# The last unit of a seven-product output matmul: products in banks of their own, the last product by row tile over two banks

## The chip, the cores and the metric

The kernel runs on one core of one Trainium2 chip. The metric is the device time of one execution in microseconds (us), as the median of nine runs; lower is better. One further execution was taken by the hardware profiler, and all durations below come from it. The engines are named as the profile names them: PE (TensorE matmuls), PEld (its weight loads), DVE (VectorE), ACT (ScalarE), POOL (GpSimd) and SP (SyncE, which here only issues DMAs).

## What is computed

```
kv  = einsum('bhsd,bhse->bhde', k, v)            # batch 8, heads 8, seq 576, head_dim 64
o   = einsum('bhsd,bhde->bhse', q, kv)
x   = o / sqrt(mean(o*o) + 1e-6) * g_norm        # -> 4608 tokens x 512
a   = x @ w_a ; b = x @ w_b                      # d_ff 1536
out = (a * b) @ w_out                            # 4608 x 512, float32
```

Only the last line, for the last 512 tokens, concerns the change.

## The kernel before, in words

**Tiling.** The 4608 tokens go in nine blocks of 512. The first block is done with plain matmuls; the eight others use a seven-product scheme (a Winograd form of Strassen's) for both halves of the feed-forward part. `wino_block` makes `a*b` for a block (lines 789 to 897, its matmuls recorded at L839), and `o_block`/`o_unit` (914 to 1109, matmuls at L1008) multiply `a*b` by `w_out`. The output work of block i-1 is mixed with the `a`, `b` work of block i. After the last block only its own output work is left; it is one unit of 512 tokens, which takes the branch `if W:` of `o_unit` (line 1065). That branch is all that the change touches.

**The unit.** Its `a*b` (tile `abt`) is cut in four: the first and second 256 tokens, and the upper and lower half of d_ff. `w_out` (tile `wo`) is cut in four too. DVE makes the sums of blocks at L993 (into `as`, or in place in `abt`); the sums of `w_out` lie in `so`. The seven products p1 to p7 are 256 x 256 outputs, each of two row tiles of 128 tokens ("subs" 0 and 1, written p3[0] and p3[1] below), each row tile six matmuls of 128x256. So a product is 12 matmuls and the unit 84. A product's two row tiles fill the two halves of a PSUM bank (512 fp32 columns). The four quarters of the output are

```
c11 = p1 + p2                    U2 = p1 + p6       U3 = U2 + p7
c22 = U3 + p5      c21 = U3 + p4      c12 = U2 + p5 + p3
```

Operands tell the products apart in the profile: p1, p2 and p5 are `wo,abt`; p4 is `so,abt`; p6 and p7 are `so,as`; p3 is `wo,as`.

**How the sums are made before the change.** Bank X holds p1; ACT copies it out (e1, L1040); p6 is accumulated in the same bank, which makes U2, and ACT copies that out (e2); then p7 is accumulated there too, which makes U3, and ACT copies that out (e3). Bank Z holds p5; ACT copies it to `u` (e5, L1076), then p3 is accumulated on it. DVE adds (function `comb`, all at L1046): c11 from bank Y and e1; c22 from bank X and `u`; c12 from bank Z and e2; c21 from two banks W[0], W[1], one per row tile, and e3. p4 alone is run by row tile. `put` issues the stores: 128 rows by 256 columns (128 KB) each, eight in the unit, on SP's or ACT's queue.

**What sets the order.** Every step is a node with an engine, a planned duration, a priority and dependences. `Plan.order` (lines 104 to 134) works through planned time: each engine takes the node of the smallest priority number among those that are ready within 0.06 us, else the one that is ready first. The result is emitted as one program per engine, and an engine runs its program strictly in that order. In this unit a product's priority is `pr + off*du`, with `off` the first argument of `prod`, and its matmuls are nodes of two (`pieces` is `NJ // 2`, 3 per row tile), so a later product can fill a gap left by an earlier one. Buffers come from rings with a limit: RO is bank 4; RX and RY share banks 0 to 3, two each; RQ and RS share banks 5 to 7, two each. `RU` gives the six `u` buffers. The unit's rings stand in the last call, lines 1153 to 1156.

**Stores.** The stores of the last unit are issued by `store` (L911). Each is one DMA over all 16 DMA engines.

Of the kernel before, what the change touches and what calls it, by code (L numbers as in the profile page):

```python
# [137 lines left out]
def kernel(  # L138
# [11 lines left out]
    nc = tc.nc  # L150
# [31 lines left out]
    NJ = FC // 2  # L182
    OP = 2
    EH = d_model // 2
# [221 lines left out]
    def mm_us(n, cols):  # L406
        return n * (cols / 2400 + 0.0025)

    def act_us(n, bias=False):
        return (0.155 if bias else 0.06) + n / 1200  # L410

    def dve_us(n):
        return (n + 65) / 960
# [7 lines left out]
        ]  # L421

    T0 = 20.0
    B5, B6, CX, CY = 5, 8, 3, 4
    TB, TURN, AHEAD = 5, 3.0, 8.0
    plan = Plan({"PE": 5.7, "DVE": 3.3, "ACT": 2.7, "SP": 5.0, "POOL": 22.5, "V": 0.0})
# [5 lines left out]
    RX, RY, RO = Ring(PB, 2), Ring(PB, 2), Ring(PO)  # L432
    RQ, RS = Ring(PA, 2), Ring(PA, 2)
    RU, RB, RAB = Ring([u_t[:, i] for i in range(6)]), Ring(b_ts), Ring(ab_ts)
# [464 lines left out]
    def store(g0, o_sb, queue=None, es=slice(0, d_model)):  # L899
        queue = queue or nc.sync  # L900
        i = 0
        while i < 128:
            b, j = divmod(g0 + i, S)
            if b < NE:
                c, sp = divmod(j, EP)
                n = min(128 - i, EP - sp)
                r0, st = b * S + EC * sp + c, EC
            else:
                n = min(128 - i, S - j)
                r0, st = b * S + j, 1  # L910
            queue.dma_start(out=out[r0 : r0 + st * (n - 1) + 1 : st, es], in_=o_sb[i : i + n, es])  # L911
            i += n
# [54 lines left out]
    def o_unit(r0, ab, muls, osum, pr, du, chunks, pieces, m, w, first, second, X, Y, Z, ob, s2, s3, s4, W):  # L967
# [3 lines left out]
        def a(lo, cols):  # L971
            return lambda js: ab.tile[:, js.start + (0 if lo else NJ) : js.stop + (0 if lo else NJ), cols]

        def sx(b):
            return lambda js: b.tile[:, js, 0:w]

        a11, a12, a21, a22 = a(1, first), a(0, first), a(1, second), a(0, second)
# [21 lines left out]
        def prod(off, ps, lhs, rhs, start, deps, takes=(), frees=(), need=None, subs=None):  # L999
            last, first = [], (subs or slice(0, m)).start  # L1000
            step = NJ // pieces
            for sub in range(m)[subs or slice(0, m)]:
                for pc in range(pieces):
                    js = range(pc * step, (pc + 1) * step)

                    def mm(sub=sub, js=js):
                        for j in js:
                            nc.tensor.matmul(  # L1008
                                ps.tile[:, sub * EH : (sub + 1) * EH],
                                lhsT=lhs(slice(j, j + 1))[:, 0, sub * 128 : (sub + 1) * 128],  # L1010
                                rhs=rhs[:, j, :],
                                start=start and sub == first and j == 0,
                                stop=j == NJ - 1,
                                skip_group_check=True,
                            )

                    nd = [muls[x] for j in js for x in (j, j + NJ) if x in muls]
                    if need is not None:
                        nd = [done[need, q] for q in range(js[0] // cj, js[-1] // cj + 1)]
                    last = [  # L1020
                        plan.add(
                            "PE", mm_us(len(js), EH), pr + off * du + 0.01 * sub, mm,
                            last + list(deps) + nd, takes if not last else (), list(frees) + [ab],
                        )
                    ]
            return last[0]

        def bank(b, subs):
            n = subs.stop - subs.start
            return b.tile[:, subs.start * EH : subs.stop * EH].rearrange("p (s e) -> p s e", s=n)  # L1030

        every = slice(0, m)

        def o(fi, h, subs=every):
            return ob.tile[:, fi * m + subs.start : fi * m + subs.stop, h * EH : (h + 1) * EH]

        def ev(off, fi, h, dep, takes=(), frees=()):
            return plan.add(
                "ACT", act_us(m * EH), pr + off * du,
                lambda: nc.scalar.copy(o(fi, h), bank(X, every)), [dep], takes, frees,  # L1040
            )

        def comb(off, fi, h, ps, deps, frees=(), subs=every, u=None):
            def add():
                other = u.tile[:, subs] if u else o(fi, h, subs)
                nc.vector.tensor_add(o(fi, h, subs), bank(ps, subs), other)  # L1046

            return plan.add(
                "DVE", dve_us((subs.stop - subs.start) * EH), pr + off * du, add, deps, (), frees
            )  # L1050

        def put(fi, subs, deps, us=0.45, queue="SP", es=slice(0, d_model)):
            q = {"SP": nc.sync, "ACT": nc.scalar}[queue]

            def go():
                for i in range(subs.start, subs.stop):
                    store(r0 + (fi * m + i) * 128, ob.tile[:, fi * m + i], q, es)

            plan.add(queue, us * (subs.stop - subs.start), pr + 7 * du, go, deps, (), [ob])

        b11, t1 = wo_t[:, 0:NJ, 0:EH], wo_t[:, 0:NJ, EH:]
        b21, b22 = wo_t[:, NJ:, 0:EH], wo_t[:, NJ:, EH:]
        t2, t3, t4 = (so_t[:, i] for i in range(3))
        n1, n2, n3, n4 = osum
        if W:
            u5 = Buf(RU)
            p1 = prod(0, X, a11, b11, True, [], [X])
            e1 = ev(0, 0, 0, p1, [ob])
            p2 = prod(1, Y, a12, b21, True, [], [Y])
            c11 = comb(1, 0, 0, Y, [p2, e1], [Y])  # L1070
            p6 = prod(2, X, sx(s2), t2, False, [e1, n2], (), [s2], 2)
            e2 = ev(2, 0, 1, p6)
            p5 = prod(3, Z, a21, t1, True, [n1], [Z], (), 1)
            e5 = plan.add(
                "ACT", act_us(m * EH), pr + 3 * du,
                lambda: nc.scalar.copy(u5.tile[:, every], bank(Z, every)), [p5], [u5],  # L1076
            )
            p7 = prod(4, X, sx(s3), t3, False, [e2, n3], (), [s3], 0)
            e3 = ev(4, 1, 0, p7)
            c22 = comb(4, 1, 1, X, [p7, e5], [X, u5], u=u5)  # L1080
            p3 = prod(5, Z, sx(s4), b22, False, [e5, n4], (), [s4], 3)
            c12 = comb(5, 0, 1, Z, [p3, e2], [Z])
            e1s, e2s = slice(0, EH), slice(EH, d_model)
            put(0, every, [c11], es=e1s)
            put(1, every, [c22], es=e2s)
            for i in range(m):
                put(0, slice(i, i + 1), [c12], queue=("SP", "ACT")[i], es=e2s)
            for i in range(m):
                subs = slice(i, i + 1)
                p4 = prod(6 + 0.1 * i, W[i], a22, t4, True, [n4], [W[i]], subs=subs)  # L1090
                c21 = comb(6 + 0.1 * i, 1, 0, W[i], [p4, e3], [W[i]], subs)
                put(1, subs, [c21], queue=("ACT", "SP")[i], es=e1s)
            return
        p1 = prod(0, X, a11, b11, True, [(wo_n, 10.6)], [X])
        e1 = ev(0, 0, 0, p1, [ob])
# [2 lines left out]
        p6 = prod(2, X, sx(s2), t2, False, [e1, n2], (), [s2], 2)  # L1098
        e2 = ev(2, 0, 1, p6)
        p5 = prod(3, Z, a21, t1, True, [e1, n1], [Z], (), 1)  # L1100
        p7 = prod(4, X, sx(s3), t3, False, [e2, n3], (), [s3], 0)
        e3 = ev(4, 1, 1, p7)
        c22 = comb(4, 1, 1, Z, [p5, e3])
        p4 = prod(5, X, a22, t4, False, [e3, n4])
        c21 = ev(5, 1, 0, p4, (), [X])
        p3 = prod(6, Z, sx(s4), b22, False, [c22], (), [s4], 3)
        c12 = comb(6, 0, 1, Z, [p3, e2], [Z])
# [6 lines left out]
    n_at = [1.2, 1.0, 1.0, 1.0, 1.0, 1.0, 1.0, 1.0, 0.5]  # L1114
    st = [T0]
    for i in range(len(lens)):
# [24 lines left out]
    for bi in range(1, nb + 1):  # L1141
# [10 lines left out]
        ab, muls = wino_block(bi, (st[bi], st[bi + 1]), wsum)  # L1152
    o_block(
        nb, ab, muls, osum, (st[nb + 1], st[nb + 1] + o_us[nb]), NJ // 2,
        (RO, RY, RY, RS, RQ), NJ // 2,
    )
    order, t = plan.order(), 5.7
    for n in order:
# [34 lines left out]
```

## Time and profile before

| what | us |
|---|---|
| median of 9 runs | 296.97 (296.83 to 298.78) |
| the profiled execution, own time | 296.97 |
| its span in the trace | 294.8 |
| last matmul run of the unit ends | 289.85 |
| last store issued | 291.32 |

A profile row reads: start, duration, engine, line of the kernel, operation, output<-inputs, shapes, count and, in brackets, how long the engine had been idle and who released it. Matmuls overlap: a row of several begins at its first and ends with its last, and neighbouring rows overlap by about 0.16 us. SPq and ACTq rows are DMA issues on those queues. `bk` is a PSUM bank, `o_sb` the output tile in SBUF that is stored from. The "chain that ended last" is followed backwards from the program's last instruction.

### The profile page before, as it was taken

Reading aid. Unit: us, or ns where it says so; the run is one execution under the profiler, and the core shown is the slowest. Engines: PE = TensorE matmul, PEld = TensorE weight load, DVE = VectorE, ACT = ScalarE, POOL = GpSimd, SP = SyncE. Lnnn points to the kernel's source line nnn. Section 1 sums busy time; section 2 is a strip of 40 time slices with the busy share of each in tenths; the row PEclk is TensorE's granted clock in tenths of the full one; section 3 lists DMA queues with packets and bytes.
Section 4 is the critical chain, followed back from the end, with each engine's and each line's share of the span. In section 5 each row is a group of like instructions: output and inputs, shape, how many; then the busy total and the mean of one; then the engine's idle time right before and its main releaser. Section 6 shows DMA issues by size and latency. Waiting matters only on the chain.

```text
span 294.8 us, 6759 instructions
## 1 busy us (share of the span) xinstructions
PE 287.4 (97%) x2648; PEld 237.7 (81%) x2648; DVE 240.1 (81%) x441; ACT 191.7 (65%) x395; POOL 77.4 (26%) x96
## 2 busy tenths in 40 slices
PE   7999999999999999999999999999999999999993
PEld 3645558965888888899988999898988888888882
DVE  5454879893987988789979999979989958798852
ACT  3756667776578677877757866786769546665420
POOL 8944830950091470470001910000000000000000
PEclk9999999999999999999999999999999999999999
DMA  8999999799999999699716999330155001200053
GB/s 180 198 199 199 197 158 166 104 168 184 198 120 170 140 174 176 50 142 203 167 30 149 147 165 167 80 145 21 37 88 164 2 0 41 104 2 0 9 172 107
DMA packets 112643, 36.26 MB, mean 123 GB/s; under 512 B 89060, under 2 KB 108516, under 8 KB 112612
## 3 DMA queue, kind: packets, MB, share of 16 engines
q0 software_dynamic: 77552, 18.44, 66.0%
q1 hardware_dynamic: 34448, 16.70, 26.7%
q10 hardware_dynamic: 612, 0.71, 0.8%
q8 instruction: 20, 0.33, 0.4%
q14 instruction: 11, 0.09, 0.1%
HBM read 37.75 MB, written 14.75 MB: 178 GB/s over the span
## 4 chain that ended last, share of the span: by engine, by line
PE 88%; DVE 4%; DMA 3%; POOL 2%; issue 1%; ACT 1%; DVEq 0%; ACTq 0%; POOLq 0%
PE bk L839 47%; PE bk L1008 24%; PE bk L387 7%; PE bk L943 3%; DMA wb_t<-in_moe_w_b_dram 3%; PE bk L624 2%; PE bk L367 1%; PE bk L353 1%; POOL as L242 1%; PE bk L539 1%; DVE c L858 1%; POOL so L242 1%; PE bk L341 1%; DVE so L746 1%; DVE o_sb L1046 1%
## 5 line engine op out<-in xcount | busy, mean ns | idle before, releaser
L858 DVE TENSOR_TENSOR c<-bk,u 128x512 f16<-128x512 f32 x144 | 96.3, 685 | 19.3 <-PE bk L839 11.8
L420 ACT COPY u<-bk 128x512 f32<-128x512 f32 x144 | 81.4, 591 | 36.5 <-PE bk L839 29.9
L839 PE MATMUL bk<-xp,wa_t 128*128 128x256 f16 x288 | 55.0, 273 | 0.1
L839 PE MATMUL bk<-xp,wb_t 128*128 128x256 f16 x288 | 55.0, 273 | 0.0
L839 PEld LDWEIGHTS <-wa_t 128*128 128x128 f16 x384 | 37.1, 98 | 5.7 <-issue 0.3
L1008 PEld LDWEIGHTS <-abt 128*128 128x128 f16 x384 | 37.5, 98 | 4.7 <-issue 0.3
L839 PEld LDWEIGHTS <-wb_t 128*128 128x128 f16 x384 | 37.6, 98 | 4.4
L1008 PE MATMUL bk<-wo_t,abt 128*128 128x256 f16 x288 | 37.2, 273 | 0.1
L839 PE MATMUL bk<-T,sb 128*128 128x256 f16 x192 | 36.7, 273 | 0.0
L839 PE MATMUL bk<-T,sa 128*128 128x256 f16 x192 | 36.6, 273 | 0.0
L420 ACT CAST c<-bk 128x512 f16<-128x512 f32 x48 | 28.0, 587 | 12.1 <-PE bk L839 11.5
L893 DVE TENSOR_TENSOR abt<-c 128x1024 f16<-128x1024 f16 x48 | 32.7, 685 | 0.9
L839 PEld LDWEIGHTS <-sb 128*128 128x128 f16 x288 | 28.2, 98 | 3.3
L839 PEld LDWEIGHTS <-sa 128*128 128x128 f16 x288 | 27.9, 98 | 3.5
L1008 PEld LDWEIGHTS <-as 128*128 128x128 f16 x288 | 28.1, 98 | 3.3
L1040 ACT COPY o_sb<-bk 128x512 f32<-128x512 f32 x31 | 18.2, 586 | 18.5 <-PE bk L1008 18.0
L376 DVE SCALAR_TENSOR_TENSOR xp<-bk,g_col,rs 128x288 f16<-128x288 f32 x40 | 20.3, 513 | 11.1 <-ACT rs L371 11.1
L1008 PE MATMUL bk<-so,as 128*128 128x256 f16 x192 | 25.2, 273 | 0.0
L371 ACT ACTIVATE rs<-bk,eps_t 128x288 f32<-128x288 f32 x40 | 20.0, 506 | 6.5 <-PE bk L367 6.3
L667 POOL DMA_DIRECT2D k_t<-in_k_dram x24 | 21.2, 899 | 0.8 <-issue 0.5
L661 POOL DMA_DIRECT2D scr<-in_q_dram x12 | 19.6, 1638 | 2.7 <-issue 1.5
L1046 DVE TENSOR_TENSOR o_sb<-bk,o_sb 128x512 f32<-128x512 f32 (+1 forms) x25 | 16.4, 664 | 3.0 <-PE bk L1008 2.3
(107 smaller groups left out, 428.2 us busy)
## 6 DMA issues: line engine op xcount, KB each, us to landing
out_dram<-o_sb SPq DMA_DIRECT2D x20, 256.0 KB, 2.7
scr<-in_q_dram POOLq DMA_DIRECT2D x12, 288.0 KB, 7.5
k_t<-in_k_dram POOLq DMA_DIRECT2D x24, 128.0 KB, 7.6
v_t<-in_v_dram POOLq DMA_DIRECT2D x6, 512.0 KB, 10.6
out_dram<-o_sb SPq DMA_DIRECT2D x18, 128.0 KB, 2.4
wa_t<-in_moe_w_a_dram POOLq DMA_DIRECT2D x6, 256.0 KB, 10.8
wb_t<-in_moe_w_b_dram POOLq DMA_DIRECT2D x6, 256.0 KB, 11.0
wo_t<-in_moe_w_out_dram POOLq DMA_DIRECT2D x2, 768.0 KB, 9.3
```

Of the source, the lines that this page charges most:

```text
L371: nc.scalar.activation(rs, self.s_ps[p, h][:, 0:HF], AF.Abs_reciprocal_sqrt, bias=eps_t)
L376: nc.vector.scalar_tensor_tensor(out=xcols(p, self.b * S + h * HF, HF), in0=self.x_ps[p, h][:, 0:HF], scalar=g_col, in1=self.rs[p, h], op0 ...
L387: nc.tensor.matmul(ps[:, 0:n], lhsT=w[:, kc, fc * 128 : (fc + 1) * 128], rhs=xcols(kc, 0, n), start=(kc == 0), stop=(kc == KC - 1),)
L420: ("ACT", act_us(n), lambda: nc.scalar.copy(*args())),
L661: nc.gpsimd.dma_start(out=scr[:, :, hl, :].rearrange("p s d -> s p d"), in_=qv[hl])
L667: nc.gpsimd.dma_start(out=kt[:, c], in_=ks[:, :, c, :])
L839: nc.tensor.matmul(ps.tile[:, i * n : (i + 1) * n], lhsT=lhs(w, sm)[:, kc, :], rhs=rhs()[:, kc, :], start=start and i == 0 and kc == 0, st ...
L858: lambda: nc.vector.tensor_add(cs(fi, h), full(ps), u.tile),
L893: nc.vector.tensor_mul(t, c[:, :, :, 0], c[:, :, :, 1])
L1008: nc.tensor.matmul(ps.tile[:, sub * EH : (sub + 1) * EH], lhsT=lhs(slice(j, j + 1))[:, 0, sub * 128 : (sub + 1) * 128], rhs=rhs[:, j, :], ...
L1040: lambda: nc.scalar.copy(o(fi, h), bank(X, every)), [dep], takes, frees,
L1046: nc.vector.tensor_add(o(fi, h, subs), bank(ps, subs), other)
```

## The change

The rings of the unit become (RO, RY, RS, RY, RS, RQ, RY), so that it has seven banks at hand instead of five.

- p7 no longer accumulates on U2. It starts in a bank V of its own (from RY), with `off` 2.5. ACT's copy e3 is gone; DVE makes U3 as bank V plus e2, into the place in `o_sb` of c21 (new node c2x).
- p5 is run by row tile, into two banks Z[0] and Z[1] (both from RS); ACT copies each half bank, 256 columns, to `u`.
- c22 becomes a DVE sum of two SBUF operands: U3 in `o_sb` and `u`.
- p4 still goes by row tile, into banks from RQ and RY, but with `off` 5 and 5.1 instead of 6 and 6.1. Its sums c21 wait for c22, since they overwrite the U3 that c22 reads.
- p3 goes last (`off` 6 and 6.1) and by row tile, each on its own Z bank; each 256-column piece of c12 is added and stored by itself. Before, c12 was one sum of 512 columns whose two stores followed it.

Matmuls: 84 before and after. Stores: eight before and after.

```
-            p7 = prod(4, X, sx(s3), t3, False, [e2, n3], (), [s3], 0)
-            e3 = ev(4, 1, 0, p7)
-            c22 = comb(4, 1, 1, X, [p7, e5], [X, u5], u=u5)
-            p3 = prod(5, Z, sx(s4), b22, False, [e5, n4], (), [s4], 3)
-            c12 = comb(5, 0, 1, Z, [p3, e2], [Z])
+            u5, V, Z = Buf(RU), W[0], [Z, W[1]]
+            W = W[2:]
...
+            e2 = ev(2, 0, 1, p6, (), [X])
+            p7 = prod(P7_AT, V, sx(s3), t3, True, [n3], [V], [s3], 0)
+            c2x = plan.add(
+                "DVE", dve_us(m * EH), pr + 4 * du,
+                lambda: nc.vector.tensor_add(o(1, 0), bank(V, every), o(0, 1)), [p7, e2], (), [V],
+            )
+            e5 = []
+            for i in range(m):
+                p5 = prod(3 + 0.1 * i, Z[i], a21, t1, True, [n1], [Z[i]], (), 1, subs=rows[i])
+                e5.append(
+                    plan.add(
+                        "ACT", act_us(EH), pr + 3 * du,
+                        lambda i=i: nc.scalar.copy(u5.tile[:, rows[i]], bank(Z[i], rows[i])),
+                        [p5], [] if i else [u5],
+                    )
+                )
+            c22 = plan.add(
+                "DVE", dve_us(m * EH), pr + 4.2 * du,
+                lambda: nc.vector.tensor_add(o(1, 1), o(1, 0), u5.tile[:, every]), [c2x] + e5, (), [u5],
+            )
...
             for i in range(m):
-                put(0, slice(i, i + 1), [c12], queue=("SP", "ACT")[i], es=e2s)
+                p4 = prod(5 + 0.1 * i, W[i], a22, t4, True, [n4], [W[i]], subs=rows[i])
+                c21 = comb(5 + 0.1 * i, 1, 0, W[i], [p4, c22], [W[i]], rows[i])
+                put(1, rows[i], [c21], queue=("ACT", "SP")[i], es=e1s)
             for i in range(m):
-                subs = slice(i, i + 1)
-                p4 = prod(6 + 0.1 * i, W[i], a22, t4, True, [n4], [W[i]], subs=subs)
-                c21 = comb(6 + 0.1 * i, 1, 0, W[i], [p4, e3], [W[i]], subs)
-                put(1, subs, [c21], queue=("ACT", "SP")[i], es=e1s)
+                p3 = prod(6 + 0.1 * i, Z[i], sx(s4), b22, False, [e5[i], n4], (), [s4], 3, subs=rows[i])
+                c12 = comb(6 + 0.1 * i, 0, 1, Z[i], [p3, e2], [Z[i]], rows[i])
+                put(0, rows[i], [c12], queue=("ACT", "SP")[i], es=e2s)
...
-        (RO, RY, RY, RS, RQ), NJ // 2,
+        (RO, RY, RS, RY, RS, RQ, RY), NJ // 2,
```

The change's name also says that q is turned in one piece. No line of the diff touches that: q of each later batch is already turned by one transposing DMA before the change (line 682).

More of the change, by code (lines that the diff above doesn't have):

```diff
@@ L423 @@
     T0 = 20.0
+    P7_AT = 2.5
     B5, B6, CX, CY = 5, 8, 3, 4
@@ L1065, in o_unit @@
         if W:
-            u5 = Buf(RU)
+            u5, V, Z = Buf(RU), W[0], [Z, W[1]]
+            W = W[2:]
+            rows = [slice(i, i + 1) for i in range(m)]
             p1 = prod(0, X, a11, b11, True, [], [X])
@@ L1071, in o_unit @@
             p6 = prod(2, X, sx(s2), t2, False, [e1, n2], (), [s2], 2)
[L1072 to L1076, printed above, removed]
-            )
-            p7 = prod(4, X, sx(s3), t3, False, [e2, n3], (), [s3], 0)
-            e3 = ev(4, 1, 0, p7)
-            c22 = comb(4, 1, 1, X, [p7, e5], [X, u5], u=u5)
-            p3 = prod(5, Z, sx(s4), b22, False, [e5, n4], (), [s4], 3)
-            c12 = comb(5, 0, 1, Z, [p3, e2], [Z])
+            e2 = ev(2, 0, 1, p6, (), [X])
[3 more added lines that the diff above has]
+                lambda: nc.vector.tensor_add(o(1, 0), bank(V, every), o(0, 1)), [p7, e2], (), [V],
+            )
+            e5 = []
[12 more added lines that the diff above has]
+            )
             e1s, e2s = slice(0, EH), slice(EH, d_model)
```

## The prediction, made before the result was known

> **What bounds the kernel now.** I read the page first, for the bound of the whole; then the chain of waits from 255 us on, for what sets the end; then the timeline of the last 14 us, for the order of products; then the stores one by one and the DMA rates of the last 5 us.
>
> ```profile
> PE 287.4 (97%) x2648; PEld 237.7 (81%) x2648; DVE 240.1 (81%) x441; ACT 191.7 (65%) x395; POOL 77.4 (26%) x96
> ```
>
> PE is busy for 97% of the span, so the body is PE's. The unit touched here comes after the body: it can give back only what lies behind the last matmul, or lose by stalling PE. The end of the chain:
>
> ```profile
> 280.46 8.09 PE bk L1008 x74
> ...
> 288.58 0.59 ACT o_sb L1040
> ...
> 289.20 1.02 DVE o_sb L1046 x2
> 290.22 0.33 DVEq L1188
> 290.55 0.60 DVE o_sb L1046
> ```
>
> The chain leaves PE at 288.56, not at PE's end. It goes over ACT's copy e3 and then a queue of four DVE sums (c22, c21[0], c21[1], c12) to 291.15. The timeline of the same stretch shows which products stand there:
>
> ```profile
> 287.07 1.47 PE L1008 MATMUL bk<-so,as 128*128 128x256 f16 x12
> 288.38 1.47 PE L1008 MATMUL bk<-wo_t,as 128*128 128x256 f16 x12
> 288.58 0.59 ACT L1040 COPY o_sb<-bk 128x512 f32<-128x512 f32 x1 [1.16 <-PE bk L1008]
> 289.20 0.69 DVE L1046 TENSOR_TENSOR o_sb<-bk,u 128x512 f32<-128x512 f32 x1 [3.80 <-ACT o_sb L1040]
> ```
>
> p7 (`so,as`) ends at 287.07 + 1.47 = 288.54, e3 starts 0.04 later, c22 0.03 after e3. p3 (`wo,as`) ends at 289.85, but its sum c12 queues behind the three others. DVE was idle for 3.8 us before c22: all four sums pile up behind e3.
>
> The stores pile up too. The first of the last six is issued at 289.91 (behind c22), the last at 291.32. The DMA rates of 289.5 to 294.3 in 40 slices of 0.12 us, then the stores issued about 291.2 to 291.3, then the lone one at 285.4:
>
> ```profile
> GB/s 0 0 0 0 0 0 0 0 0 0 137 350 316 239 290 350 358 324 359 316 316 350 358 324 342 358 333 325 350 333 128 0 0 0 0 0 0 0 0 0
> ```
> ```profile
> DMA to landing us min/median/max: 2.1/2.2/2.3
> ```
> ```profile
> L911 SPq DMA_DIRECT2D out_dram<-o_sb x1: 332/332/332, 285.4 to 285.4; - x1
> ...
> DMA to landing us min/median/max: 1.7/1.7/1.7
> ```
>
> Bytes run without a gap from 290.7 to 293.2, at about 335 GB/s. So the last store lands 2.3 us after its issue, at 293.6, against 1.7 for one with the queue to itself: the tail is a full DMA queue, and its start at c22 matters as much as the last issue. After the landing come about 1.2 us of closing instructions to 294.8, and 2.17 us outside the span make 296.97. Neither is touched.
>
> **The order after the change.** Priorities are in planned time, so I followed the planner's rule by hand. Which gaps a later product fills can be read before the change:
>
> ```profile
> 280.95 0.60 PE L1008 MATMUL bk<-so,abt 128*128 128x256 f16 x4
> 281.39 0.60 PE L1008 MATMUL bk<-wo_t,abt 128*128 128x256 f16 x4
> 281.83 0.38 PE L1008 MATMUL bk<-so,abt 128*128 128x256 f16 x2
> 282.05 0.60 PE L1008 MATMUL bk<-wo_t,abt 128*128 128x256 f16 x4
> ```
>
> These are p4, p2, p4, p5: the last mul of `a*b` (L893) ends only at 282.45, and PE fills up with what needs it not. In the new order p5 has the smaller priority number and its RS banks are free, so it takes p4's slots; p7[0] takes p5's slot at 282.05, when RY has its second bank. Then p1 (8 matmuls), p2 (8), p7[0] (2), p6 (12, from 284.67 as now), p7[1] (6), p5[0] and p5[1] (2 each, to 287.07), p4[0], p4[1], p3[0], p3[1] (6 each). That is 84 matmuls in the same 84 slots of 0.109 us, the last run again ending at 289.85, if PE waits nowhere. The waits that are new on PE, with those who would queue behind them (all the unit's later matmuls, as PE runs in order): p5's first pieces need DVE sums in `abt` that ended by 275.3; p7[0] needs its RY bank, which the former unit's c12 left at 281.85 (margin 0.20, and p5 stood in that slot with the same need); p7's last pieces need the L993 sum that ended at 282.91 (margin 1.5); p3[0] needs e5[0] (below, margin 1.0). I cost them at nothing; each us of stall would cost one.
>
> **Costs part by part**, from these rows:
>
> ```profile
> L640 ACT CAST kvd<-bk 64x256 bf16<-64x256 f32 x6 | 2.2, 368 | 0.1
> ...
> L1046 DVE TENSOR_TENSOR o_sb<-bk,o_sb 128x256 f32<-128x256 f32 x2 | 0.7, 414 | 0.0
> L1046 DVE TENSOR_TENSOR o_sb<-bk,u 128x512 f32<-128x512 f32 x1 | 0.7, 691 | 3.8 <-ACT o_sb L1040 3.8
> ```
>
> Removed: e3, 0.59 us of ACT, all of it in the chain. Added: c2x, a DVE sum of a bank and SBUF, 0.69; one more 256-column piece on each of ACT and DVE.
>
> - c2x: p7[1] ends at 286.80, e2 at 286.77 (as now), so it runs from 286.84 to 287.53, in DVE's 3.8 us of idleness.
> - e5: a 256-column copy on ACT has no row of its own shape. It lies between half of the 512-column copy, 0.29, and the whole, 0.59. I take the 0.37 of the 64x256 cast, the row of the same width. p5[0] ends at 287.01: e5[0] 287.05 to 287.42, e5[1] to 287.79 (to 288.23 at 0.59 each, still inside the slack found below).
> - c22 from two SBUF operands in fp32 is not in the trace. The nearest row has 512 columns with one bank operand, 0.69; the 256-column row (0.414) bounds it from below. I take 0.69: 287.82 to 288.51.
> - c21[0], c21[1]: p4[1] ends at 288.54. Before, two such pieces started 0.33 apart, so c21[0] runs 288.54 to 288.96, c21[1] 288.87 to 289.29. This wait of c21 for c22 is new; behind it on DVE stand c21 and c12 alone.
> - c12[0]: p3[0] ends at 289.20, so 289.24 to 289.65. c12[1]: 289.89 to 290.30.
>
> So the last sum ends at 290.30 instead of 291.15, 0.41 + 0.04 behind the last matmul. c22 has slack: four more sums behind it need 3 x 0.33 + 0.41, so it could end 0.4 later before c12[1] moved.
>
> [...] two halves cost 2 x 0.33 of DVE against 0.61 from c22's start to the next, 0.05 more in throughput. [...] By the rows the piece behind the last matmul is 0.41, and DVE has room for the 0.05. I follow the rows: the split is worth 0.27, not a loss.
>
> **The stores.** Issues, each just behind its sum (SP's second 0.38 behind its first): c22 on SP 288.54 and 288.92, c21[0] on ACT 288.99, c21[1] on SP 289.32, c12[0] on ACT 289.68, c12[1] on SP 290.33. ACT has no copy left to delay. Data began 0.79 after the first issue before (289.91 to 290.70), and 131 KB at 335 GB/s takes 0.39. One behind another: 289.33 to 289.72, then 290.11, 290.50, 290.89, 291.28, 291.67. The queue now drains as fast as it fills, and the last landing is 0.4 behind the last byte (293.61 against 293.2 before), at about 292.1.
>
> Sum: 293.6 - 292.1 = 1.5 us. The profiled execution's own time is 296.97, equal to the median: 296.97 - 1.5 = **295.5**.
>
> [...]
>
> **The rivals.**
> 1. *Only the issue moves.* The last store still takes 2.3: 296.97 - 0.99 = 296.0. For it: the stores at 290.3 took 2.0 to 2.2 with only one or two ahead. Against: 1.7 on an empty queue.
> 2. *PE pays it back.* One of the new waits on PE (V's bank, with 0.2 us of margin, is the tightest) stalls everything by about 1.3 us, or c22 comes late by that and 0.4 more: 296.8, no change. Against: p5 passed in the same slot with no gap, and the e5 margin is 1.0. That the order doesn't come out as I derived it belongs here; p3 and p4 swapped would leave the tail the same.
> 3. *Slower: the sums wait for stores in flight.* c21 and c12 write `o_sb` while c22's stores read it. If writes to one tile waited for its stores, c21[1] would wait for the landing of c22's second store (288.92 + 1.8 = 290.7), end at 291.15, its store land at 293.0, and c12 follow that: its second piece ends at 293.8, its store lands at 295.6, 2.0 later than now: 299.0. It decides when c21[1] starts after 290.2. Against: now c12 starts at 290.47 with three stores from this tile in flight, so regions are told apart.
>
> **How the numbers follow.** 0.2% (0.6 us) is about what a measurement of this kernel can tell from no change. Main case 0.64 (295.2 to 295.75); rival 1 0.20 (295.75 to 296.3); rival 2 0.09; rival 3 0.07. Faster 0.84, within 0.2% 0.09, slower 0.07. The range 295.2 to 296.3 takes in the first two; the low end has the last landing at 1.5 behind its issue, less than any store took.
>
> **What would show it.** Right: no ACT copy behind p7; DVE sums spread from 286.8 to 290.3, the last a 128x256 starting 0.04 behind PE; PE still ending 84 slots after 280.5, with no gap; the last store issued at 290.3 and landing at 292.1. Wrong: a gap in PE's row of the unit, c21[1] after 290.2, a landing 2.3 behind the last issue, or an earlier stage that moved though the diff leaves it alone.

## The result and the profile after

The changed kernel takes 295.77 us as the median of nine runs, against 297.0 for the kernel before on the same chips: ratio 0.9956, 95% interval 0.9946 to 0.9966, so 0.44% faster. In two later sets it took 295.48 and 295.60 beside 297.02 and 297.01. The forecast was 295.5 with a range of 295.2 to 296.3. The profiled execution of the changed kernel took 295.24, with a span of 293.1.

The page's first rows, as before the change: PE is as busy as it was, and DVE has the two instructions more that were counted.

```profile
PE 287.8 (98%) x2648; PEld 237.8 (81%) x2648; DVE 241.1 (82%) x443; ACT 191.1 (65%) x395; POOL 77.3 (26%) x96
```

The chain that ended last now stays on PE until its last matmul and ends with one short sum; line numbers have moved by one, so L1009 is the former L1008.

```profile
280.14 9.40 PE bk L1009 x86
289.54 0.02 issue
289.56 0.42 DVE o_sb L1047
```

The timeline of the unit gives the order of the products (columns: start, duration, engine, line, operation, output<-inputs, shapes, count, idle before; rows that don't bear on the order are left out):

```profile
280.63 1.25 PE L1009 MATMUL bk<-wo_t,abt 128*128 128x256 f16 x10
281.72 0.60 PE L1009 MATMUL bk<-so,as 128*128 128x256 f16 x4
282.16 2.13 PE L1009 MATMUL bk<-wo_t,abt 128*128 128x256 f16 x18
283.45 0.59 ACT L1041 COPY o_sb<-bk 128x512 f32<-128x512 f32 x1 [4.65 <-PE bk L1009]
284.12 2.35 PE L1009 MATMUL bk<-so,as 128*128 128x256 f16 x20
284.38 0.69 DVE L1047 TENSOR_TENSOR o_sb<-bk,o_sb 128x512 f32<-128x512 f32 x1 [0.42 <-PE bk L1009]
285.85 0.59 ACT L1041 COPY o_sb<-bk 128x512 f32<-128x512 f32 x1 [1.81 <-PE bk L1009]
286.31 0.60 PE L1009 MATMUL bk<-wo_t,abt 128*128 128x256 f16 x4
286.56 0.69 DVE L1079 TENSOR_TENSOR o_sb<-bk,o_sb 128x512 f32<-128x512 f32 x1 [1.49 <-PE bk L1009]
286.72 0.65 ACT L1087 COPY u<-bk 128x256 f32<-128x256 f32 x2 [0.29 <-PE bk L1009]
286.74 1.47 PE L1009 MATMUL bk<-so,abt 128*128 128x256 f16 x12
287.40 0.69 DVE L1093 TENSOR_TENSOR o_sb<-o_sb,u 128x512 f32<-128x512 f32 x1
288.05 1.47 PE L1009 MATMUL bk<-wo_t,as 128*128 128x256 f16 x12
288.20 1.13 DVE L1047 TENSOR_TENSOR o_sb<-bk,o_sb 128x256 f32<-128x256 f32 x3
289.56 0.42 DVE L1047 TENSOR_TENSOR o_sb<-bk,o_sb 128x256 f32<-128x256 f32 x1 [0.23 <-PE bk L1009]
```

These are 80 of the unit's 84 matmuls; its first four stand at 279.10. By the kinds of operands the order is the one that was worked out, in slots with no gap: p5[0], p2 and p5[1] (10), p7[0] (4), p5[1], p1 and p2 (18), p7[0], p6 and p7[1] (20), the rests of p5 (4), then p4 and p3. How a row divides among products of the same kind is not in the row itself, but what follows each product starts where this division has it end: e1 behind p1 (283.45), c11 behind p2 (284.38), e2 behind p6 (285.85). c2x (L1079) and c22 (L1093) now run beside p4's matmuls. Three sums are done before the last matmul, and DVE waits 0.23 for the last one.

The DMA rates of 287.5 to 292.3 in slices of 0.12 us, and the store issued last, at 290.05:

```profile
GB/s 0 0 0 0 0 0 0 0 0 0 0 0 222 350 341 171 196 358 324 359 324 358 324 359 324 359 299 367 341 359 324 350 137 9 0 0 0 0 0 0
```
```profile
DMA to landing us min/median/max: 1.8/1.8/1.8
```

The bytes begin at 288.9, 0.6 ahead of the last matmul's end; before, they began 0.9 behind it. They take about as long as before (2.6 against 2.5) and end at 291.5. The last store lands at 291.86.

I measure the end by three distances from the end of the last matmul run: the last issue, the last landing (the *tail*), and the *closing* from there to the end of the span.

| profiled execution | last matmul ends | last issue | tail | closing |
|---|---|---|---|---|
| before | 289.85 | 1.47 | 3.76 | 1.22 |
| after | 289.52 | 0.53 | 2.34 | 1.23 |

So 1.42 of the 1.73 us between these two profiled executions is the tail. The other 0.33 arises before the code that was changed. In both kernels PE waits for the first half of w_b at 16 us, and that load came at different times (PE and its weight load, before and then after):

```profile
16.39 0.11 PEld L387 LDWEIGHTS <-wb_t 128*128 128x128 f16 x2 [0.77 <-DMA wb_t<-in_moe_w_b_dram]
16.39 0.60 PE L387 MATMUL bk<-xp,wb_t 128*128 128x512 f16 x2 [0.28 <-DMA wb_t<-in_moe_w_b_dram]
```
```profile
16.07 0.11 PEld L387 LDWEIGHTS <-wb_t 128*128 128x128 f16 x2 [0.47 <-DMA wb_t<-in_moe_w_b_dram]
16.07 0.61 PE L387 MATMUL bk<-xp,wb_t 128*128 128x512 f16 x2
```

Matmul by matmul, the two executions differ by 0.33 from here on, up to the end.

### The profile page after: what moved, and what is told of

Same layout as the page of the kernel before. It is cut to its first block, busy times and chain, and to the rows that moved or that the text cites. A ratio compares the mean times of both kernels' runs of the same rounds, so it can differ in the third digit from the quotient of the medians.

```text
span 293.1 us, 6763 instructions
## 1 busy us (share of the span) xinstructions
PE 287.8 (98%) x2648; PEld 237.8 (81%) x2648; DVE 241.1 (82%) x443; ACT 191.1 (65%) x395; POOL 77.3 (26%) x96
## 4 chain that ended last, share of the span: by engine, by line
PE 92%; DVE 3%; DMA 1%; issue 1%; ACTq 0%; ACT 0%
PE bk L840 48%; PE bk L1009 25%; PE bk L387 7%; PE bk L944 3%; PE bk L625 2%; PE bk L353 2%; PE bk L367 2%; DMA g_row<-in_g_norm_dram 1%; PE bk L310 1%; PE bk L341 1%; PE bk L540 1%; PE bk L325 1%; DVE c L859 1%; DVE so L747 1%; DVE T L807 1%
## 5 line engine op out<-in xcount | busy, mean ns | idle before, releaser
L1009 PEld LDWEIGHTS <-abt 128*128 128x128 f16 x384 | 37.5, 98 | 4.6 <-issue 0.3
L1009 PE MATMUL bk<-wo_t,abt 128*128 128x256 f16 x288 | 37.0, 273 | 0.1
L1009 PEld LDWEIGHTS <-as 128*128 128x128 f16 x288 | 28.1, 98 | 3.3
L1041 ACT COPY o_sb<-bk 128x512 f32<-128x512 f32 x30 | 17.6, 586 | 17.3 <-PE bk L1009 16.4
L1009 PE MATMUL bk<-so,as 128*128 128x256 f16 x192 | 25.2, 273 | 0.0
```

The source lines that it names most:

```text
L1009: nc.tensor.matmul(ps.tile[:, sub * EH : (sub + 1) * EH], lhsT=lhs(slice(j, j + 1))[:, 0, sub * 128 : (sub + 1) * 128], rhs=rhs[:, j, :], ...
```

## The experiments

My theory (below "tail theory"): bringing p7 forward in a bank of its own starts c22 early, which takes the sums and the stores from behind the last matmul; cutting the last product adds to it. The rivals: the cut alone does it; the copy e3 leaving ACT does it; the stores' gain is the issue alone; a part of the gain comes from the start of the kernel. Each kernel was timed in five rounds beside the kernel before. The edits are shown shortened. A run's name is written in full (e2_p7_on_U2), so that it isn't taken for ACT's copies e1, e2, e3 and e5.

**The changed kernel again**

> The changed kernel once more, as a base beside the others on the same chip. Tail theory (p7 brought forward in a bank of its own starts c22 about 1.4 us earlier, which empties the queues of DVE sums and of stores; the cut of the last sum adds a little): the last store lands 2.3 to 2.4 us behind the end of the last matmul run, against 3.76 before, and the median is 1.2 to 1.4 below the kernel before. Start theory (part of the gain is the 0.33 us by which PE waited less for w_b at 16 us, outside the changed code): the tail is the same, but the median comes to 1.4 or less below, and the 0.33 comes and goes from one execution to the next.

Measured: 295.48 against 297.02 (ratio 0.9948, interval 0.9929 to 0.9967), tail 2.34, last matmul at 289.82. PE met w_b at 16.36 here, as before the change at 16.39, and the span is 1.45 shorter with the 1.42 in the tail. So the gain of the change is in the tail, and the start comes and goes without it.

**p3 whole again (e1_whole_p3)**

```
-            e5 = []
-            for i in range(m): p5 = prod(3 + 0.1 * i, Z[i], ...); e5.append(copy of 256 columns)
+            p5 = prod(3, Z, a21, t1, True, [n1], [Z], (), 1)
+            e5 = ...                                   # one copy of 512 columns
...
+            p3 = prod(6, Z, sx(s4), b22, False, [e5, n4], (), [s4], 3)
+            c12 = comb(6, 0, 1, Z, [p3, e2], [Z])      # one sum, then two stores
```

> The changed kernel with p5, p3 and c12 whole again in one bank (p7 keeps its own bank and place). Tail theory: the last sum is a 512-column one of 0.68 instead of 0.42, its two stores go out together 0.75 behind the last matmul, and the last of them lands about 2.8 behind it: 0.45 above the changed kernel, about 0.9 below before. Cut theory (the row tiles of the last product are what gains): the gain is lost, landing about 3.7 behind, within 0.2 of the kernel before.

Measured: 296.13 (ratio 0.9964, 0.9952 to 0.9977), tail 2.92. Its timeline, at the end:

```profile
288.25 0.69 DVE L1088 TENSOR_TENSOR o_sb<-o_sb,u 128x512 f32<-128x512 f32 x1 [0.74 <-ACT u L1084]
288.30 1.47 PE L1009 MATMUL bk<-wo_t,as 128*128 128x256 f16 x12
289.05 1.46 DVE L1047 TENSOR_TENSOR o_sb<-bk,o_sb 128x256 f32<-128x256 f32 x3
```

The last row merges two pieces of c21 and the 512-column c12, which starts 0.04 behind the last matmul and takes 0.69. The cut theory falls: 0.84 of the 1.42 stay without the cut. With p7 early, the cut of p5, p3 and their copy and sum is worth 0.58: 0.23 in the last issue (0.76 instead of 0.53), and 0.35 in the lag behind it, 2.16 instead of 1.81: the last two stores go out at one moment, and c22's stores, which waited for the 512-column copy of p5, are 0.6 later.

**p7 on U2 again (e2_p7_on_U2)**

```
-            p7 = prod(P7_AT, V, sx(s3), t3, True, [n3], [V], [s3], 0)
-            c2x = plan.add("DVE", ...)
+            p7 = prod(P7_AT, X, sx(s3), t3, False, [e2, n3], (), [s3], 0)
+            e3 = ev(4, 1, 0, p7)
...
+            c22 = comb(4.2, 1, 1, X, [p7, e3] + e5, [X, u5], u=u5)
```

> The changed kernel with p7 accumulated on U2 in bank X again and copied out by ACT (e3), c22 added from the bank; p3 and c12 still last and by row tile. p7 then waits for e2 and falls back to the 12 slots just ahead of p3. Tail theory: c22 starts only 0.3 behind the sum of p3's first row tile, four sums and all stores pile up again, the last sum ends about 1.4 behind the last matmul and the last store lands 3.8 behind it: the gain is gone, within 0.2 of before. Cut theory: the gain stays, landing at 2.4 to 2.6.

Measured: 296.77 (ratio 0.9988, 0.9981 to 0.9996), tail 3.86.

```profile
287.01 1.47 PE L1009 MATMUL bk<-so,as 128*128 128x256 f16 x12
288.32 1.47 PE L1009 MATMUL bk<-wo_t,as 128*128 128x256 f16 x12
288.52 0.59 ACT L1041 COPY o_sb<-bk 128x512 f32<-128x512 f32 x1 [1.54 <-PE bk L1009]
289.24 0.42 DVE L1047 TENSOR_TENSOR o_sb<-bk,o_sb 128x256 f32<-128x256 f32 x1 [3.91 <-PE bk L1009]
289.58 0.68 DVE L1047 TENSOR_TENSOR o_sb<-bk,u 128x512 f32<-128x512 f32 x1
290.18 1.08 DVE L1047 TENSOR_TENSOR o_sb<-bk,o_sb 128x256 f32<-128x256 f32 x3
```

With p7 in bank X it waits for the copy e2 and is back in the slot ahead of p3; DVE is idle for 3.91 and then has five sums in a row. The cut by itself gains nothing in the tail. The median is 0.25 lower than before although the tail is 0.10 longer. The record shows where this lies: the median span is 294.9 in both, but in this run the time outside the span is 1.88 us on average, against 2.16 for the kernel before. It is 1.98 in e1_whole_p3 and 1.96 in e3_p7_late too, and 2.1 to 2.2 in all others, the changed kernel among them. Why is open; so for these three the tail is the better measure than the median.

**p7 in its own bank, but late (e3_p7_late)**

```
-    P7_AT = 2.5
+    P7_AT = 5.5
```

> The changed kernel with one number changed: p7's place 5.5 instead of 2.5, so that p7 keeps its own bank and DVE's sum for U3 but runs just ahead of p3. Tail theory: U3 is ready 0.7 behind p7, c22 starts at about the last matmul's end less 0.3, the last sum ends 1.6 behind the last matmul, the last store lands 3.8 behind: the gain is gone. Copy theory (what gains is that ACT's copy e3 left the chain): the gain stays for the most part, landing at 2.4 to 2.9.

Measured: 296.97 (ratio 0.9993, 0.9981 to 1.0006), tail 4.00. No ACT copy stands behind p7 here, and the gain is gone all the same:

```profile
289.07 0.69 DVE L1079 TENSOR_TENSOR o_sb<-bk,o_sb 128x512 f32<-128x512 f32 x1 [3.24 <-PE bk L1009]
289.87 0.42 DVE L1047 TENSOR_TENSOR o_sb<-bk,o_sb 128x256 f32<-128x256 f32 x1
290.21 0.68 DVE L1093 TENSOR_TENSOR o_sb<-o_sb,u 128x512 f32<-128x512 f32 x1
290.81 1.08 DVE L1047 TENSOR_TENSOR o_sb<-bk,o_sb 128x256 f32<-128x256 f32 x3
```

The copy theory falls: DVE's sum for U3 takes no less than ACT's copy did (0.69 against 0.59). What counts is the place of p7 on PE; the own bank is what permits that place, as e2_p7_on_U2 shows from the other side.

**p3 and p4 exchanged (e6_p4_last)**

```
-  p4 = prod(5 + 0.1 * i, W[i], ...)      p3 = prod(6 + 0.1 * i, Z[i], ...)
+  p4 = prod(6 + 0.1 * i, W[i], ...)      p3 = prod(5 + 0.1 * i, Z[i], ...)
```

> The changed kernel with the places of p3 and p4 exchanged: p3's two row tiles go ahead of p4's second one, and the last sum is a piece of c21. Tail theory: any product whose sum is one 256-column piece is as good at the end; landing 2.3 to 2.4 behind the last matmul, no difference from the changed kernel. Order theory (p3 at the end is what matters, since p4 had been filling gaps): 0.2 or more above it, or a gap in PE where p3 waits for ACT's copies of p5.

Measured: 295.71 (ratio 0.9957, 0.9943 to 0.997), tail 2.33, no gap in the unit.

```profile
288.67 1.47 PE L1009 MATMUL bk<-wo_t,as 128*128 128x256 f16 x12
289.98 0.82 PE L1009 MATMUL bk<-so,abt 128*128 128x256 f16 x6
290.84 0.42 DVE L1047 TENSOR_TENSOR o_sb<-bk,o_sb 128x256 f32<-128x256 f32 x1 [0.23 <-PE bk L1009]
```

Whether p3 or p4 is last is of no account. The profiled execution of this kernel (296.51) lost 1 us at 194, behind a DMA that brings `xp` back (it took 2.70, to 193.27, and ACT waited 0.9 for it; in r_after ACT had no such wait): such a stall far from the change is almost as large as the change.

**Stores: issue or queue?** Four runs.

> The kernel before with the two stores of c22 left out (these 256 rows by 256 columns of the output are not written), nothing else. The last issue moves by 0.14, since SP is free sooner. Queue theory: four stores instead of six behind the sums; the last lands 3.3 behind the last matmul instead of 3.76, 0.4 to 0.5 below before. Issue theory: 0.14 below before.

The edit to the kernel before:

```
-            put(1, every, [c22], es=e2s)
```

Measured: 296.7 against 297.02 (ratio 0.9988, 0.998 to 0.9996), tail 3.42. The last issue moved by 0.14, as both theories have it; the landing moved by 0.34. The lag from issue to landing shrank from 2.29 to 2.09. The issue theory allows no such thing; the queue theory expected about 0.1 more.

> The changed kernel with the same sums at the same times, but the stores of c22 and c21 are held until the sum c12[0] is done, so that five stores go out together about 0.2 ahead of the last matmul's end. The last store is issued 0.1 to 0.2 later than in the changed kernel. Queue theory (the last landing is set by when the stores begin, 0.39 us each at 335 GB/s): the bytes begin about 0.7 behind the last matmul, six stores take 2.3, the last lands about 3.4 behind it, 1.0 to 1.1 above the changed kernel. Issue theory (each store lands a fixed time behind its issue): 0.1 to 0.2 above it.

```
-            put(1, every, [c22], es=e2s)
...
+                if i == 0:
+                    put(1, every, [c22, c12], es=e2s)
+                    for h in range(m):
+                        put(1, rows[h], [held[h], c12], queue="ACT", es=e1s)
```

Measured: 295.59 (ratio 0.9955, 0.9943 to 0.9967), tail 2.33, and c22's stores issued at 1.41 and 1.03 ahead of the last matmul's end, as in the changed kernel. The edit held nothing: a dependence given to the planner sets the order of emission, but the wait in the program follows from the data, and a store of c22 needs only c22. So this run tells nothing of the queue; it shows only that c21[1]'s store can change queues for nothing.

> The mend of the held stores: c12[0]'s store is cut in two halves of 64 rows, one at the head of SP's queue and one at the head of ACT's, and the stores of c22 and c21 stand behind them in the queues, the last store (c12[1]) at the end of ACT's. All sums stay where they are. Stores begin 0.12 ahead of the last matmul's end; with 0.4 per issue the last is issued at about 1.1 to 1.3 behind it (0.53 in the changed kernel). Queue theory: bytes begin at 0.7, 0.79 MB take 2.35, the last lands at about 3.4. Issue theory: issue plus 1.8, so 2.9 to 3.1.

```
+            plan.add("SP", 1.3, pr + 7 * du, line(nc.sync, 0, ((1, 0, e2s), (1, 1, e2s))), [c120, c12], (), [ob])
+            plan.add("ACT", 1.7, pr + 7 * du, line(nc.scalar, 1, ((1, 0, e1s), (1, 1, e1s), (0, 1, e2s))), [c120, c12], (), [ob])
```

Measured: 297.29 (ratio 1.0009, 0.9999 to 1.0018), tail 4.03. The stores were held this time, and all the gain was lost with every sum in its place. But the issues themselves became slow (0.45 to 0.80 for all but the last, while both queues issued a 64-row and then 128-row stores), so the last one came at 1.87, and with the lag of 1.8 the issue theory too gives 3.7. Both theories are short of the measured 4.03, and the run doesn't separate them.

What does is one recipe for all kernels whose late stores are whole and issued at the usual pace: a store's turn begins 0.79 behind its issue or at the end of the turn ahead of it and takes 0.39, and the last landing comes 0.6 behind the end of the last turn (0.4 as I had it, and 0.2 added to fit these runs):

| kernel | last issue | recipe | measured tail |
|---|---|---|---|
| before | 1.47 | 3.79 | 3.76 |
| after | 0.53 | 2.33 | 2.34 |
| e1_whole_p3 | 0.76 | 2.93 | 2.92 |
| e2_p7_on_U2 | 1.93 | 3.84 | 3.86 |
| e3_p7_late | 2.06 | 3.97 | 4.00 |
| e5_before_4stores | 1.33 | 3.49 | 3.42 |
| e9_last_semaphore (below) | 0.53 | 2.75 | 2.68 |

The lags run from 1.81 to 2.29, and a queue explains the tails to within 0.07. A fixed lag doesn't. The last row parts the two theories most plainly, though its run was made for another purpose: its sums and its last issue stand where they do in the changed kernel, but c22's stores go out 0.4 later. The issue theory gives 2.34 for it. Its last store took 2.2 to land, not 1.8:

```profile
L912 SPq DMA_DIRECT2D out_dram<-o_sb x1: 333/333/333, 290.3 to 290.3; - x1
...
DMA to landing us min/median/max: 2.2/2.2/2.2
```

The missing 0.2 lies in the bytes, not behind them. In the kernel before, the six stores' bytes begin 0.39 apart on average, so 0.39 is right for a turn; but the last store's own bytes run for 0.54, overlapping those of the store ahead of it, and they begin 0.83, not 0.79, behind the first issue. The landing comes 0.35 behind the last byte.

> The changed kernel with the last store cut in two of 64 rows, issued side by side on SP's and ACT's queues. If part of the 1.8 us from issue to landing is the making of the store's 128 row pieces by one queue (an issue takes 0.33 to 0.43), it lands 0.1 to 0.2 sooner; if it is the way to memory and back, nothing changes or the second queue adds 0.05 to 0.1.

```
+            for qn, qe, a in (("SP", nc.sync, 0), ("ACT", nc.scalar, 64)):
+                ...  qe.dma_start(out=out[g0 : g0 + 64, e2s], in_=ob.tile[a : a + 64, m - 1, e2s])
```

Measured: 296.05 (ratio 0.9974, 0.9957 to 0.9991), tail 2.73, so 0.39 worse. The two half stores, and their landings:

```profile
L1110 ACTq DMA_DIRECT2D out_dram<-o_sb x1: 553/553/553, 290.6 to 290.6; - x1
L1110 SPq DMA_DIRECT2D out_dram<-o_sb x1: 472/472/472, 290.6 to 290.6; - x1
...
DMA to landing us min/median/max: 2.0/2.1/2.2
```

Each half took longer to issue than the whole store (0.33), and landed later. Both guesses were wrong. Whether the 64 rows or the side-by-side issue makes it slow is not settled. The side-by-side issue alone doesn't make the issues slow: in e1_whole_p3 two whole stores issued at the same moment took 0.33 and 0.38. But the second of them also landed late, 2.16 behind its issue.

**A shorter closing.** In the traces so far the span goes on for 1.16 to 1.30 after the last landing. Part of it is SP waiting for the eight completion semaphores of the stores in a fixed order; the last store has the third in the kernels before and after (1.22 and 1.23), and five waits long met follow, 0.06 apart.

> The changed kernel with c11, stored 4 us ahead of the end, cut in seven small stores instead of two. It moves no sum and no late store; but the completion semaphores go round among eight, and five more stores put the last one on the eighth instead of the third. After the last landing SP still walks through five waits that have long been met, 0.06 each (0.3 of the 1.2 us of closing). If that walk is on the path, the span ends 0.3 sooner behind the last landing (0.92 instead of 1.22), about 0.3 below the changed kernel; if the walk is hidden, or the small stores delay c22's, nothing or a loss of up to 0.2.

```
-            put(0, every, [c11], es=e1s)
+            for i, a, n in ((0, 0, 32), (0, 32, 32), (0, 64, 32), (0, 96, 32), (1, 0, 64), (1, 64, 32), (1, 96, 32)):
+                nc.sync.dma_start(out=out[g0 : g0 + n, e1s], in_=ob.tile[a : a + n, i, e1s])
```

Measured: 295.66 (ratio 0.9963, 0.9942 to 0.9984), closing 0.93 as expected, but tail 2.68: seven issues of 0.34 to 0.58 kept SP until 0.98 ahead of the last matmul's end, and c22's first store went out 0.4 late. Gain and loss cancel (0.30 and 0.35).

> The mend of the last-semaphore kernel: the five extra stores are made 8 us ahead of the end, by cutting the last store of the unit before into six pieces (SP has 2.5 us to spare there), so that c11's and all later stores go as in the changed kernel, and the last store again has the eighth completion semaphore. If the two effects are separate: tail from the last matmul to the last landing 2.34 as in the changed kernel, closing 0.93 instead of 1.22, 0.3 below the changed kernel beside it. If cutting stores costs again: the tail above 2.4.

```
+                    if r0 == n_tok - 2 * N0 and (fi, i) == (0, 1):
+                        for c0, c1 in ((0, 32), (32, 64), (64, 80), (80, 96), (96, 112), (112, 128)):
+                            q.dma_start(out=out[g0 + c0 : g0 + c1, es], in_=row[c0:c1, es])
```

> The changed kernel beside it: tail 2.34, closing 1.22, median 1.2 to 1.5 below the kernel before.

Measured, side by side: 295.26 (ratio 0.9952, 0.9932 to 0.9972) for this kernel, tail 2.32, closing 0.93; 295.60 (0.995, 0.9934 to 0.9965) for the changed kernel, tail 2.33, closing 1.22. The traces show the 0.3; the medians agree with it, but their intervals overlap, so by the times alone it is not shown that this kernel is the faster one. Two earlier traces, in which the place moved for other reasons, bear the cause out: the last landing has the second semaphore in e1_whole_p3, with a closing of 1.30, and the fourth in e8_queued_stores, with 1.16. That is about 0.06 for each place. (In e5_before_4stores it has the eighth, but the store with the first landed only 0.19 ahead of it, so that SP still had the whole walk to do, and the closing is 1.16.)

## Why the prediction was right, step by step

- **The order on PE**: right, as far as the rows tell products apart. PE's last run ends with no gap; c2x, e5 and c22 lie beside p4 as placed. The tightest wait (V's bank, 0.20) cost nothing. One count was loose: "84 slots after 280.5" are 86 matmuls, the former unit's last six and 80 of this unit.
- **The sums**: the last one takes 0.425 and starts 0.04 behind PE, forecast 0.41 and 0.04. Small terms were off and cancelled: ACT's two copies took 0.37 each as taken, but began 0.27 apart, not 0.37, so c22 came 0.09 sooner; c21[0] began 0.10 behind the end of c22, not 0.03.
- **c22 from two SBUF operands**: 0.693, taken as 0.69.
- **The stores**: forecast 1.5, measured 1.42; in part this is luck. I set a recipe for the new landing against a measured old one. The recipe is 0.2 short for both, which did not cancel; recipe against recipe gives 3.59 - 2.13 = 1.46. That the c22 store went out 0.09 sooner than forecast made up for half of it. What was short is above all the last store's own run of bytes: 0.54, where the sum has 0.39. So the 0.79 MB of the kernel before took 2.51 us, 313 GB/s, where 335 was taken for all of it.
- **The cut of the last product**: right to make, but its price was off. I gave it 0.27, from the rows before: c12 as one sum took 0.68, a 256-column piece 0.41. It is worth 0.58 (e1_whole_p3), since it also parts the last two stores and, by the half copies of p5, brings c22's stores forward by 0.6; and without the early p7 it is worth nothing (e2_p7_on_U2).
- **Rival 1** kept the lag of 2.3 that the last store had before. The forecast, 290.33 to 292.1, has 1.8, an estimate of mine near the 1.7 of the store at 285.4. The measured lag is 1.81, and rival 1 is out; the lag is not fixed at 1.81 either (the table above). The median of the first set, 0.27 above the forecast, might look like it; but the tail is 2.33 to 2.34 in three profiled executions of the changed kernel, and the repeats have 295.48 and 295.60. The difference is elsewhere than in the tail.
- **Rivals 2 and 3**: PE has no gap, and c21[1] starts 0.98 ahead of PE's end, at 288.54, when c22's two stores are issued (288.12 and 288.50) and not landed (the second lands at 290.34), so here a write to one part of the tile did not wait for a store in flight from another.

## What to carry to other kernels

At the end of a kernel bound by PE, look at what the last matmuls release: put the product with the longest way behind it (copy, sum, sum, stores) early enough that other products' matmuls cover it, and pay with a PSUM bank of its own if an accumulation pins its place. Then let the last product release as little as possible; here the cut paid 0.58 with p7 early and nothing with p7 late, where sums and stores queued. In this kernel late stores had to be counted as a queue with a start (tails to within 0.07), not as issues with a fixed lag (1.81 to 2.29). Compare a recipe with the same recipe applied to the kernel before.

## What the hardware did that I had not expected

- Two stores of 64 rows issued side by side on SP's and ACT's queues took 0.47 and 0.55 to issue and 2.0 to 2.2 to land; the one store of 128 rows that they replace took 0.33 and 1.8.
- In the changed kernel c22's two stores, alone on SP's queue, are issued 0.38 apart, but their bytes begin 0.49 apart, and the row shows a dip between them (171 and 196 GB/s). From then on SP's and ACT's queues take turns, the bytes begin 0.37 to 0.39 apart, and the row stays at 299 to 367.
- The place of the last store's completion semaphore has a price of about 0.06 us: the closing is 1.30 with the second of eight, 1.22 with the third, 1.16 with the fourth and 0.93 with the eighth.
- The time to the first use of w_b at 16 us moved by 0.3 between profiled executions of kernels that are alike up to there, and all that followed kept the difference.
